# Attention, then a rational feed-forward, on one core: four phases of w made in place, one DMA queue, and a reciprocal by Ln, Exp and a Newton step

## The chip, the core and the metric

One core of one Trainium2 chip runs the whole program. The metric is the device time of one execution in microseconds (us); lower is better. TensorE (PE) multiplies, VectorE (DVE), ScalarE (ACT) and GpSimd (POOL) work on tiles, and SyncE (SP) issues DMA transfers. Each engine takes its instructions in the order in which the program holds them.

## The reference, cut to what matters

Four batches, twelve heads, 448 positions, head size 64; then 1792 tokens through a feed-forward of width 768 to 2048 to 768.

```python
scores = scale * np.matmul(q, k.transpose(0, 1, 3, 2))
scores = np.einsum('bhij,hg->bgij', scores, w_pre)
scores = scores - np.max(scores, axis=-1, keepdims=True)
attn = np.exp(scores)
attn = attn / (np.sum(attn, axis=-1, keepdims=True) + 1e-09)
attn = np.einsum('bhij,hg->bgij', attn, w_post)
x = matmul(attn, v)            # then regrouped to 1792 x 768
h = x @ w_in
P = a[0] + a[1] * h + a[2] * h2 + a[3] * h3
Q = 1.0 + np.abs(b[0]) * np.abs(h) + np.abs(b[1]) * h2
g = P / (Q + 1e-06)
out = g @ w_out
```

## The kernel before, in words

The program has two parts. A small planner (`Plan`, `add`) gets every step with its engine, an estimated duration, what it depends on and a due time `at`; it runs through them once in simulated time, and the order it finds is the order in which each engine gets its instructions. Rings (`Ring`, `R[...]`) stand for buffers that are used again. Nothing of the planner runs on the chip: there, an engine simply waits at its next instruction until what that one needs is there.

**Attention.** There are 16 row tiles, four to a batch. For a tile, `put_qk` multiplies q and k for six pairs of heads (L451), ScalarE or VectorE copies the scores to `st`, and one DMA for each head (`shuffle`, L467, `d<-st`, 210 KB, twelve to a tile) lays them out in `d` so that the heads can be mixed by a matmul. There are two buffers of `d`. `put_pre` mixes the heads (L518, the first matmul that needs the whole shuffled tile), VectorE takes the maxima (L525), ScalarE the exponentials (L534), GpSimd scales the second mixing matrix (L554). `put_post` mixes again (L594), VectorE transposes (L610), `put_av` multiplies by v (L653) and splits the result into a high and a low half, `xs` (L667). At the end of a batch `xs` is stored to a scratch, `x_scr` (L671). The shuffles of a tile run while the tile before is being worked on. Shuffles stand on SyncE's queue; the loads of q (L352), k (L364) and v (L632) of all but the first tiles, and the stores of x, stand on ScalarE's (`bulk(second, ...)`).

**The weights.** w_in and w_out come as one array w of 64-bit floats: 16 rows (f) of 128 x 1536 values. `put_w` makes a quarter of a row (a *piece*, 128 x 384, 64 in all): a load `cr` on SyncE (L380), Abs on ScalarE (L385), a clamp on GpSimd (L390), three integer steps on VectorE (L394, L399, L405), a high half on ScalarE (cast `co`, L235), a low half on GpSimd (L416), and a store to the scratch `w_scr` on SyncE (L419). 36 pieces are due during attention (`W1 = 36`), 28 after it. `put_load_w` loads a whole row of both halves, 1.5 MB, from the scratch (L764); eight rows have room at a time.

**Feed-forward.** 64 units: a unit is one row f of w and one batch b. `put_unit` multiplies x by w_in (18 matmuls, L799, into one of two `ps_s` banks) and later adds g times w_out to six banks (18 matmuls, L873). Between them ScalarE makes four values (L810, L813, L816, L820), VectorE the polynomial P (L823, L826), the denominator (L830), its reciprocal (L833) and the quotient (L836); g is split into a high half (cast, L235 or L237) and a low half (L846). There are two phases of eight rows; within a phase the four batches take turns of eight units. At the end of a turn the six banks are copied to `o` and stored in `o_scr`, or in the second phase added to what was stored (L910) and sent out (L917). x of a batch that is not at hand is loaded again (L780).

What sets the order of the units, of the x tiles held and of the pieces:

```python
    turns = [(0, 3), (0, 0), (0, 1), (0, 2), (1, 2), (1, 1), (1, 0), (1, 3)]
    units = [(c, b, f) for c, b in turns for f in range(CH)]
    held = [0, 1, 2, 3, 3, 2, 4, 5]
    homes = {1: (0, "x"), 2: (1, "xs"), 3: (2, "x"), 4: (0, "x"), 5: (3, "xs")}
```

```python
        if i < W1:
            put_w(f, c, at=T0 + 10.0 + (tau[first[NT - 1]] - T0 - 30.0) * i / W1)
        else:
            put_w(f, c, at=END1 + 26 * UNIT * (i - W1) / (len(pieces) - W1))
```

## Time and profile before

| what | value |
|---|---|
| median of 3 runs | 952.78 us (951.53 to 957.07) |
| profiled execution, its own time | 955.4 us |
| span of the profiled execution | 953.6 us |
| mean granted TensorE clock | 0.958 |
| TensorE matmul, weight load busy | 850.2 us (89%), 649.6 us (68%) |
| VectorE busy | 751.7 us (79%) |
| ScalarE busy | 415.2 us (44%) |
| GpSimd busy | 358.2 us (38%) |
| DMA | 175.32 MB, mean 184 GB/s |

Times are from the start of the span. Busy time is a mean over parts with different limits, so the table alone does not tell what a part waits for. Matmuls are pipelined and their ends modelled; a granted clock of 1.00 is full speed. In rows of waits, what stands behind `<-` is what ended the wait, as inferred from the semaphores; where several things were awaited it is the one that came last.

### The profile page before, as it was taken

What the parts mean: (1) busy time and instruction counts of PE and PEld (TensorE: products, weight loads), DVE (VectorE), ACT (ScalarE), POOL (GpSimd) and SP (SyncE); (2) the same over time, 40 slices, a digit from 0 to 9 for tenths busy, and PEclk for the clock granted to TensorE, in tenths of its full rate; (3) what the DMA queues carried; (4) which work ended last, traced back from release to release, by engine and by line L of the source; (5) the groups of instructions that cost most, each with busy time, mean ns of one, the idle gap of its engine ahead of it and who ended that gap; (6) DMA issues with size and microseconds to landing.
All of it is one profiled execution on the core that took longest, in us unless ns stands there. A gap on an engine that the chain in (4) does not pass through costs nothing.

```text
span 953.6 us, 26592 instructions
## 1 busy us (share of the span) xinstructions
PE 850.2 (89%) x11088; PEld 649.6 (68%) x11088; DVE 751.7 (79%) x1158; ACT 415.2 (44%) x928; POOL 358.2 (38%) x472
## 2 busy tenths in 40 slices
PE   3588889879877998897899899899999999999996
PEld 1245445444535555554689799799999999999995
DVE  4467768768856888686898999999788787887975
ACT  1245544545534656454435645544344233233420
POOL 2255455546435665243525645451111112121110
PEclk9789899999989999899999999999999999999998
DMA  7577768867887677547796536521555230420212
GB/s 239 182 218 217 230 209 282 267 182 237 249 277 225 204 219 248 195 149 276 245 424 240 186 119 232 174 84 39 203 213 190 102 112 20 174 97 1 77 40 77
DMA packets 68119, 175.32 MB, mean 184 GB/s; under 512 B 6336, under 2 KB 47392, under 8 KB 65312
## 3 DMA queue, kind: packets, MB, share of 16 engines
...
q8 instruction: 87, 1.43, 0.6%
...
## 4 chain that ended last, share of the span: by engine, by line
PE 54%; DMA 17%; DVE 16%; issue 6%; POOL 3%; ACT 3%; SPq 1%; POOLq 0%; DVEq 0%; ACTq 0%
PE ps_s L799 17%; PE ps_t L873 11%; DMA d<-st 7%; PE ps_a L873 6%; PE ps_t L518 5%; PE ps_a L594 5%; PE ps_s L451 5%; PE ps_t L653 4%; DVE rc L833 4%; DMA w_scr<-co 3%; DMA kk<-in_k 2%; DVE aa L610 2%; DMA x_scr<-xs 2%; DVE cg L399 2%; POOL cm L390 1%
## 5 line engine op out<-in xcount | busy, mean ns | idle before, releaser
L846 POOL TENSOR_TENSOR g<-rc,g 128x448 fp32r<-128x448 f32 x63 | 76.7, 1218 | 312.6 <-DVE g L237 201.0
L833 DVE RECIPROCAL rc<-sq 128x448 f32<-128x448 f32 x64 | 188.5, 2945 | 1.2
L873 PE MATMUL ps_t<-g,w 128*128 128x448 f32 x768 | 180.2, 366 | 0.1
L518 PE MATMUL ps_t<-d,kpre 64*64 64x448 f32 x720 | 105.6, 605 | 57.8 <-DMA d<-st 24.8
L873 PEld LDWEIGHTS ps_t<-g,w 128*128 128x128 f32 x768 | 144.1, 188 | 12.4 <-POOL g L846 0.5
L594 PEld LDWEIGHTS ps_a<-e,krs 64*32 64x32 f32 x5760 | 81.4, 110 | 89.3 <-issue 39.8
L525 DVE TENSOR_REDUCE nm<-ps_t 128x1 f32<-128x448 f32 x180 | 104.4, 607 | 39.0 <-PE ps_t L518 38.2
L390 POOL TENSOR_SCALAR cm<-cm 128x384 f32<-128x384 f32 x64 | 98.4, 1540 | 78.0 <-ACT cm L385 71.5
L799 PE MATMUL ps_s<-x,w 128*128 128x448 f32 x576 | 123.8, 369 | 3.7 <-DVE m L826 3.7
L799 PE MATMUL ps_s<-xs,w 128*128 128x448 f32 x576 | 122.7, 366 | 3.8 <-DVE m L826 3.5
L534 ACT ACTIVATE e<-ps_t,nm 128x448 f32<-128x448 f32 x180 | 113.0, 636 | 27.8 <-DVE nm L525 19.4
L451 PE MATMUL ps_s<-kk,q 64*64 64x448 f32 x736 | 113.0, 608 | 12.6 <-DMA kk<-in_k 6.7
L610 DVE STREAM_TRANSPOSE aa<-ps_a 128x448 f32<-128x448 f32 (+1 forms) x184 | 106.8, 615 | 19.8 <-PE ps_a L594 19.2
L810 ACT ACTIVATE m<-ps_s,a_sb 128x448 f32<-128x448 f32 x64 | 46.3, 724 | 171.8 <-PE ps_s L799 171.7
L594 PE MATMUL ps_a<-e,krs 64*32 64x112 f32 x5760 | 109.3, 272 | 13.1 <-issue 4.9
L799 PEld LDWEIGHTS ps_s<-x,w 128*128 128x128 f32 x576 | 109.4, 190 | 13.3 <-DVE m L826 4.1
L799 PEld LDWEIGHTS ps_s<-xs,w 128*128 128x128 f32 x576 | 107.7, 188 | 14.2 <-DVE m L826 4.6
L554 POOL TENSOR_SCALAR krs<-kpost,rr 128x64 f32<-128x64 f32 x180 | 89.5, 510 | 68.2 <-DVE rr L545 56.3
L873 PE MATMUL ps_a<-g,w 128*128 128x448 f32 x384 | 97.8, 366 | 0.0
L653 PE MATMUL ps_t<-aa,vv 128*64 128x120 f32 (+1 forms) x1536 | 83.0, 262 | 2.7 <-DVE aa L610 1.6
L416 POOL TENSOR_TENSOR co<-cm,co 128x384 fp32r<-128x384 f32 x64 | 68.3, 1069 | 44.6 <-ACT co L235 44.3
L235 ACT COPY st<-ps_s 120x448 f32<-120x448 f32 (+1 forms) x104 | 52.7, 532 | 73.4 <-PE ps_s L451 60.7
...
## 6 DMA issues: line engine op xcount, KB each, us to landing
...
```

What stands on the lines that cost most here:

```text
L390: nc.gpsimd.tensor_scalar(out=m, in0=m, scalar1=F64_MIN, scalar2=F64_MAX, op0=ALU.max, op1=ALU.min)
L451: nc.tensor.matmul(box["s"][hh][i0:i1, 0:S], lhsT=Q[T][d, pr, i0:i1], rhs=K[b][d, pr, :], start=True, stop=True)
L518: nc.tensor.matmul(box[r if nt == 2 else 0]["t"][64 * c:64 * c + 64, 0:S], lhsT=kpre[p], rhs=Dt[T][p, kb + c if nt == 2 else kb, :], start ...
L525: nc.vector.tensor_reduce(out=nm, in_=box[r]["t"][:, 0:S], axis=AX.X, op=ALU.max, negate=True)
L534: nc.scalar.activation(e, box[r]["t"][:, 0:S], AF.Exp, bias=box[r]["nm"], accum_out=box[0]["sm"][:, r:r + 1])
L554: eng.tensor_scalar_mul(box[r]["kr"], kpost, rr)
L594: nc.tensor.matmul(banks[c]["p"][BT * q_:BT * (q_ + 1), j0:j0 + JT], lhsT=box[r]["kr"][p, m_, :], rhs=box[r]["e"][p, q_ * JT:(q_ + 1) * JT ...
L610: nc.vector.transpose(o, src)
L653: nc.tensor.matmul(t[64 * hf:64 * hf + 64, pr * n:(pr + 1) * n], lhsT=V[b][:, j, g, :], rhs=A[T][:, 3 * (g // G6) + j, 0:n // G5, G5 * (g ...
L799: nc.tensor.matmul(h[:, 0:S], lhsT=W[fi][:, wi, kk * 128:(kk + 1) * 128], rhs=x[:, kk // 3, xj, kk % 3, :], start=(n == 0), stop=(n == 3 * ...
L833: nc.vector.reciprocal(new("rc"), box["vv"])
L873: nc.tensor.matmul(O[key][:, 0:S], lhsT=W[fi][:, wi, DM + m * 128:DM + (m + 1) * 128], rhs=box["g"][:, gi, :], start=(f == 0 and n == 0), ...
```

## The change

Four things are edited.

- **Phases.** The feed-forward has four phases of four rows of w (`PH = 4`); a turn has four units, there are 16 turns, and partial sums go through `o_scr` three times instead of once. x tiles are loaded nine times instead of five.
- **Pieces.** Only the 16 pieces of the first phase are made during attention and go through the scratch. The other 48 are due one to a unit, a phase ahead of use, and are written straight into the buffer of the row (`W[f]`), without store and load.
- **Queue.** All loads of q, k, v and all stores of x go to SyncE's queue, k in six parts instead of three, v in four instead of two, x in twelve to a batch instead of four.
- **Reciprocal.** Ln and Exp(-x) on ScalarE give a first value r, and two VectorE instructions make r * (d * r - 2), the negative of a Newton step; the coefficients a are negated once to make up for the sign. One table load for Ln is placed ahead of the first unit.

```diff
+PH = 4
-    w_scr = [dram.tile([128, 2, WC], F32, name=f"w_scr{f}") for f in range(NF)]
+    w_scr = [dram.tile([128, 2, WC], F32, name=f"w_scr{f}") for f in range(PH)]
...
-    b1_op = add("act", 0.15, lambda: nc.scalar.activation(b1_sb, b_sb[:, 1:2], AF.Abs), [ab_ld], at=40.0)
+    def fit_ab():
+        nc.scalar.activation(b1_sb, b_sb[:, 1:2], AF.Abs)
+        nc.scalar.activation(a_sb, a_sb, AF.Copy, scale=-1.0)
...
-            (nc.scalar if T > 1 else nc.sync).dma_start(out=Q[T], in_=q[T])
+            nc.sync.dma_start(out=Q[T], in_=q[T])
...
-                (nc.scalar if b else nc.sync).dma_start(out=K[b][:, i * n:(i + 1) * n], in_=k[b, :, i * n:(i + 1) * n])
+                nc.sync.dma_start(out=K[b][:, i * n:(i + 1) * n], in_=k[b, :, i * n:(i + 1) * n])
...
         def hi(eng):
-            t = sb["co"].tile([128, 2, CV], F32R, tag="co", name="co")
+            if f < PH:
+                t = sb["co"].tile([128, 2, CV], F32R, tag="co", name="co")
+            else:
+                if c == 0:
+                    W[f] = sb["wr" if f % CH < NR else "wl"].tile([128, 2, WC], F32R, tag="w", name=f"w{f}")
+                t = W[f][:, :, sl]
...
+        if f < PH:
+            home = [R["co"].take()]
+        elif c == 0:
+            home = [op_begin if f % CH < NR else op_rest, w_use[f - CH] if f >= CH else None]
+        else:
+            home = []
...
-                (nc.scalar if b else nc.sync).dma_start(out=V[b][:, 2 * j:2 * j + 2], in_=v[b, :, 2 * j:2 * j + 2])
+                nc.sync.dma_start(out=V[b][:, j], in_=v[b, :, j])
...
-                nc.scalar.dma_start(out=x_scr[b][:, hv, hl], in_=Xs[b][:, hv, hl].bitcast(F32))
+                nc.sync.dma_start(out=x_scr[b][:, hv, hl, p], in_=Xs[b][:, hv, hl, p].bitcast(F32))
...
-        put_k(b, 3, at=tau[first[4 * b - 2]] - 40.0, gap=12.0)
+        put_k(b, 6, at=tau[first[4 * b - 2]] - 40.0, gap=7.0)
...
-    pieces = [(f, c) for f in range(NF) for c in range(NCV)]
-    for i, (f, c) in enumerate(pieces):
-        if i < W1:
-            put_w(f, c, at=T0 + 10.0 + (tau[first[NT - 1]] - T0 - 30.0) * i / W1)
-        else:
-            put_w(f, c, at=END1 + 26 * UNIT * (i - W1) / (len(pieces) - W1))
+    for i in range(PH * NCV):
+        put_w(i // NCV, i % NCV, at=T0 + 10.0 + (tau[first[NT - 1]] - T0 - 40.0) * i / (PH * NCV))
...
+    orders = [(3, 0, 1, 2), (2, 1, 0, 3)]
+    turns = [(c, b) for c in range(NF // PH) for b in orders[c % 2]]
+    units = [(c, b, f) for c, b in turns for f in range(PH)]
+    held = [0, 1, 2, 3, 3, 2, 4, 5, 5, 4, 6, 7, 7, 6, 8, 9]
...
         def cubic():
+            if u == 0:
+                nc.scalar.preload_act_table_set("natural_log_exp_and_others")
...
-        def rec():
-            nc.vector.reciprocal(new("rc"), box["vv"])
+        def log():
+            nc.scalar.activation(box["ua"], box["vv"], AF.Ln)
+
+        def seed():
+            nc.scalar.activation(new("rc"), box["ua"], AF.Exp, scale=-1.0)
+
+        def step1():
+            nc.vector.tensor_mul(box["vv"], box["vv"], box["rc"])
+
+        def step2():
+            nc.vector.scalar_tensor_tensor(
+                out=box["rc"], in0=box["vv"], scalar=-2.0, in1=box["rc"], op0=ALU.add, op1=ALU.mult)
...
+    for u in range(len(units)):
+        i = u + PH * NCV
+        if i < NF * NCV:
+            put_w(i // NCV, i % NCV, at=END1 + UNIT * u + 2.0, since=END1 + UNIT * u - 6.0)
```

Some lines of the changed kernel are called by their number below: L852 is `step1`, L855 `step2`, L846 and L849 are Ln and Exp there, L936 the addition of partial sums.

Where the instructions move is shown at two places. The first is SyncE's queue in the middle of the attention part, in the kernel before (`d<-st` is a shuffle, `cr` a load and `w_scr` a store of a piece; L467, L380, L419):

```order
L467 DMA d<-st 10x12x448 x6
L380 DMA cr<-in_w 128x768
L467 DMA d<-st 10x12x448 x3
L419 DMA w_scr_121<-co 256x1x384
L467 DMA d<-st 10x12x448
L380 DMA cr<-in_w 128x768 x2
L419 DMA w_scr_121<-co 256x1x384
```

And in the changed kernel (`vv`, `kk` and `q` are parts of v, k and q; L489 is the shuffle there):

```order
L654 DMA vv<-in_v 128x768
L387 DMA cr<-in_w 128x768
L489 DMA d<-st 10x12x448 x4
L369 DMA kk<-in_k 128x448
L431 DMA w_scr_117<-co 256x1x384
L489 DMA d<-st 10x12x448 x2
L357 DMA q<-in_q 128x768
L489 DMA d<-st 10x12x448 x2
L369 DMA kk<-in_k 128x448
L431 DMA w_scr_117<-co 256x1x384
```

Between the shuffles there now stand parts of q, k and v, and fewer pieces. Before, those loads stood in ScalarE's order, between its own work, here also from the middle of the attention part:

```order
L632 DMA vv<-in_v 128x1536
L385 ACTIVATE cm<-cr 128x384
L534 ACTIVATE e,sm<-ps_t,nm 128x448 x2
L352 DMA q<-in_q 128x768
L235 CAST co<-cm 128x384
```

In the changed kernel ScalarE's order holds no load of q, k or v and no store of x.

The second place is VectorE's order in the feed-forward, with pieces among the units. Before, in the first phase:

```order
L833 RECIPROCAL rc<-sq 128x448
L394 TENSOR_SCALAR cm<-cm 128x384
L836 SCALAR_TENSOR_TENSOR rc<-m,a_sb,rc 128x448
L399 SCALAR_TENSOR_TENSOR cg<-cr,cm 128x384
L823 TENSOR_TENSOR m<-m,ps_s 128x448
L405 SCALAR_TENSOR_TENSOR cm<-cr,cg 128x384
```

In the changed kernel, in the second phase:

```order
L406 SCALAR_TENSOR_TENSOR cg<-cr,cm 128x384
L412 SCALAR_TENSOR_TENSOR cm<-cr,cg 128x384
L852 TENSOR_TENSOR sq<-sq,rc 128x448
L401 TENSOR_SCALAR cm<-cm 128x384
L855 SCALAR_TENSOR_TENSOR rc<-sq,rc 128x448
L406 SCALAR_TENSOR_TENSOR cg<-cr,cm 128x384
L859 SCALAR_TENSOR_TENSOR rc<-m,a_sb,rc 128x448
L412 SCALAR_TENSOR_TENSOR cm<-cr,cg 128x384
```

The reciprocal is gone, two instructions stand ahead of the quotient (L859) that both need `rc` of ScalarE, and steps of pieces stand between them.

## Rows read from the trace of the kernel before

**Rows 1.** Busy time by stretch: each engine (instructions), TensorE clock, DMA share, GB/s

```profile
core 0: us, PE busy (x) PEld busy (x) DVE busy (x) ACT busy (x) POOL busy (x), PEclk, DMA share, GB/s
30.00:466.00 436.00, 368.92 (x8728) 213.44 (x8721) 323.01 (x690) 218.23 (x578) 217.30 (x357) 0.93 0.71 224
390.00:420.00 30.00, 29.73 (x780) 18.05 (x776) 24.70 (x54) 17.22 (x47) 12.38 (x28) 1.00 0.50 154
466.00:602.00 136.00, 131.44 (x634) 119.98 (x635) 127.91 (x147) 69.83 (x129) 65.67 (x50) 0.99 0.68 251
602.00:946.00 344.00, 340.22 (x1672) 313.22 (x1670) 288.25 (x307) 123.62 (x216) 69.73 (x58) 1.00 0.29 104
```

**Rows 2.** Groups of TensorE, 30 to 466 us: busy, mean ns | idle before, releasers

```profile
L518 PE MATMUL ps_t<-d,kpre 64*64 64x448 f32 x719 | 105.6, 605 | 46.4 <-DMA d<-st 13.5 <-issue 12.3 <-DMA cr<-in_w 11.1
```

**Rows 3.** Time line of TensorE, 170 to 205 us: start, length, [idle before <-releaser]

```profile
170.87 2.38 PE L518 MATMUL ps_t<-d,kpre 64*64 64x448 f32 x8 [5.09 <-DMA w_scr<-co]
...
175.36 0.98 PE L518 MATMUL ps_t<-d,kpre 64*64 64x448 f32 x8
...
204.52 0.88 PE L518 MATMUL ps_t<-d,kpre 64*64 64x448 f32 x2 [4.09 <-issue]
```

**Rows 4.** Waits of SyncE's queue, 20 to 466 us: total us, times, longest

```profile
SPq L380 <- DVE cm L405: 25.1, 6, 14.2
SPq L467 <- DMA kk<-in_k: 24.1, 6, 6.8
SPq L467 <- DMA vv<-in_v: 21.7, 5, 7.4
...
SPq L467 <- DMA x_scr<-xs: 14.9, 4, 7.3
SPq L467 <- DMA q<-in_q: 13.9, 3, 5.7
```

**Rows 5.** Chain that ended last, 154 to 171 us: start, length, what

```profile
154.27 6.41 DMA kk<-in_k
...
160.75 5.28 DMA d<-st
...
166.53 4.31 DMA w_scr<-co
```

**Rows 6.** Groups, ScalarE's first step of a piece, 30 to 466 us

```profile
L385 ACT ACTIVATE cm<-cr 128x384 f32<-128x384 f32 x43 | 23.9, 558 | 70.8 <-DMA cr<-in_w 58.2 <-POOL co L416 12.5
```

**Rows 7.** Groups of VectorE, 470 to 602 us

```profile
L833 DVE RECIPROCAL rc<-sq 128x448 f32<-128x448 f32 x18 | 53.0, 2944 | 0.4
L830 DVE TENSOR_TENSOR sq<-sq,ua 128x448 f32<-128x448 f32 x18 | 13.7, 760 | 0.1
L399 DVE SCALAR_TENSOR_TENSOR cg<-cr,cm 128x384 int32<-128x384 int32 x16 | 12.9, 806 | 0.3
L826 DVE SCALAR_TENSOR_TENSOR m<-m,a_sb,ps_s 128x448 f32<-128x448 f32 x18 | 12.1, 672 | 0.0
L836 DVE SCALAR_TENSOR_TENSOR rc<-m,a_sb,rc 128x448 f32<-128x448 f32 x17 | 11.4, 672 | 0.1
L823 DVE TENSOR_TENSOR m<-m,ps_s 128x448 f32<-128x448 f32 x18 | 10.8, 601 | 5.1 <-ACT ua L816 5.1
L405 DVE SCALAR_TENSOR_TENSOR cm<-cr,cg 128x384 int32<-128x384 int32 x16 | 10.4, 653 | 0.1
L394 DVE TENSOR_SCALAR cm<-cm 128x384 int32<-128x384 int32 x16 | 9.4, 589 | 1.9 <-POOL cm L390 1.9
```

**Rows 8.** Line L830, 470 to 602 us: shortest/median/longest ns

```profile
L830 DVE TENSOR_TENSOR sq<-sq,ua x18: 609/622/1187, 472.8 to 599.9; 128x448 f32<-128x448 f32 x18
```

**Rows 9.** Groups of VectorE, whole span: additions to o, casts of g

```profile
L237 DVE CAST g<-rc 128x448 fp32r<-128x448 f32 x36 | 14.1, 393 | 3.2
L910 DVE TENSOR_TENSOR o<-ps_t,o 128x448 f32<-128x448 f32 x16 | 9.9, 621 | 2.8 <-PE ps_t L873 2.6
```

**Rows 10.** Groups of ScalarE, whole span: attention's Exp, the unit's Identity

```profile
L534 ACT ACTIVATE e<-ps_t,nm 128x448 f32<-128x448 f32 x180 | 113.0, 636 | 27.8 <-DVE nm L525 19.4 <-DVE rr L545 8.0
L820 ACT ACTIVATE sq<-sq,c_sb,b_sb 128x448 f32<-128x448 f32 x64 | 49.2, 768 | 0.0
```

More of the change, by code (lines that the diff above doesn't have):

```diff
@@ L351, in load @@
             Q[T] = sb["q"].tile([128, H // 2, TQ], F32, tag="q", name="q")
-            (nc.scalar if T > 1 else nc.sync).dma_start(out=Q[T], in_=q[T])
-        q_ld[T] = bulk(T > 1, 0.63, load, [R["q"].take()], at=at, nbytes=128 * H // 2 * TQ * 4)
+            nc.sync.dma_start(out=Q[T], in_=q[T])
+        q_ld[T] = bulk(0.63, load, [R["q"].take()], at=at, nbytes=128 * H // 2 * TQ * 4)
     def put_k(b, parts, at, gap=0.8):
@@ L368, in put_k, with put_w @@
         for i in range(parts):
-            k_ld[b].append(bulk(b > 0, 0.5, load(i), [free] + k_ld[b][:1], at=at + gap * i, nbytes=128 * n * S * 4, since=at + gap * i - 4.0))
+            k_ld[b].append(bulk(0.45, load(i), [free] + k_ld[b][:1], at=at + gap * i, nbytes=128 * n * S * 4, since=at + gap * i - 4.0))
     w_done = {f: [] for f in range(NF)}
-    def put_w(f, c, at):
+    w_ld, w_use = {f: [] for f in range(NF)}, {f: [] for f in range(NF)}
+    W = {}
+    def put_w(f, c, at, since=0.0):
         sl = slice(c * CV, (c + 1) * CV)
@@ L419, in store @@
             nc.sync.dma_start(out=w_scr[f][:, :, sl], in_=box["o"].bitcast(F32))
[L421 removed]
+        ld = add("sp", 0.45, load, [R["cr"].take()], at=at - 5.0, extra=dma(128 * CV * 8), since=max(since, at - 14.0))
         o1 = add("act", act(CV), mag, [ld, R["cm"].take()], at=at)
[L423 removed]
+        o2 = add("pool", 1.54, clamp, [o1], at=at)
         o3 = add("dve", dve(CV, True), shift, [o2], at=at)
[L425 to L426 removed]
+        o4 = add("dve", 0.59, top, [o3, R["cg"].take()], at=at)
+        o5 = add("dve", 0.57, tail, [o4], at=at)
         R["cg"].uses[-1].append(o5)
         R["cr"].uses[-1].append(o5)
[L429 removed]
+        if f < PH:
[4 more added lines that the diff above has]
+            home = []
+        o6 = add(copies(CV, on=ON["w_hi"]), 0, hi, [o5] + [x for x in home if x], at=at, after=w_ld[f][:1] if f >= PH else ())
         o7 = add(subs(CV, on=ON["w_lo"]), 0, lo, [o6], at=at)
         R["cm"].uses[-1].append(o7)
[L432 to L434 removed]
+        if f < PH:
+            o8 = add("sp", 0.57, store, [o7], at=at, extra=dma(128 * CV * 8), late=2.0)
+            R["co"].uses[-1].append(o8)
+            w_done[f].append(o8)
+        else:
+            w_ld[f].append(o6)
+            w_ld[f].append(o7)
     qk_op, shuf, evac = {}, {}, {}
@@ L636, in put_v @@
         v_ld[b] = []
-        for j in range(NJ // 2):
-            v_ld[b].append(bulk(b > 0, 0.63, load(j), [free] + v_ld[b][:1], at=at + 10.0 * j, nbytes=2 * 128 * H * D * 4, since=at + 10.0 * j))
+        for j in range(NJ):
+            v_ld[b].append(bulk(0.63, load(j), [free] + v_ld[b][:1], at=at + 8.0 * j, nbytes=128 * H * D * 4, since=at + 8.0 * j))
     Xs = {}
@@ L689, in put_av @@
         if T % 4 == 3:
-            for i in range(2):
-                o = bulk(True, 0.6, store(i), x_done[b, hv], at=at + 5.0 + 5.0 * (2 * i + hv),
-                         nbytes=128 * 3 * S * 4, late=1.0, since=at + 4.0 + 5.0 * (2 * i + hv))
+            for i in range(6):
+                o = bulk(0.45, store(i // 3, i % 3), x_done[b, hv], at=at + 5.0 + 1.6 * (2 * i + hv),
+                         nbytes=128 * S * 4, late=2.0, since=at + 4.0 + 1.6 * (2 * i + hv))
                 x_st.setdefault(b, []).append(o)
@@ L748, in mixed_attention_then_rational_ffn @@
     op_rest = add("sp", 0.0, rest, [left_ops, op_begin], at=-100.0)
-    turns = [(0, 3), (0, 0), (0, 1), (0, 2), (1, 2), (1, 1), (1, 0), (1, 3)]
-    units = [(c, b, f) for c, b in turns for f in range(CH)]
-    held = [0, 1, 2, 3, 3, 2, 4, 5]
-    homes = {1: (0, "x"), 2: (1, "xs"), 3: (2, "x"), 4: (0, "x"), 5: (3, "xs")}
-    W, X, O = {}, {}, {}
-    w_ld, x_ld, m2_op, o_ev = {}, {}, {}, {}
-    w_use = {f: [] for f in range(NF)}
+    orders = [(3, 0, 1, 2), (2, 1, 0, 3)]
+    turns = [(c, b) for c in range(NF // PH) for b in orders[c % 2]]
+    units = [(c, b, f) for c, b in turns for f in range(PH)]
+    held = [0, 1, 2, 3, 3, 2, 4, 5, 5, 4, 6, 7, 7, 6, 8, 9]
+    homes = {n: (turns[held.index(n)][1], "xs" if n in (2, 5, 6, 9) else "x") for n in range(1, 10)}
+    X, O = {}, {}
+    x_ld, m2_op, o_ev = {}, {}, {}
     x_use = {0: R["xs"].uses[B - 1]}
@@ L888, in put_unit @@
         w_use[fi].append(prev)
-        if f == CH - 1:
+        if f == PH - 1:
             for m0 in range(0, KD, 2):
@@ L933, in put_unit @@
                     R["xo"].uses[-1].append(s_)
-                    if not c:
-                        o_st.setdefault(b, []).append(s_)
+                    o_st.setdefault((c, b), []).append(s_)
     for f in range(NR):
         put_load_w(f, at=END1 - 30)
-    for f in range(NR, CH):
+    for f in range(NR, PH):
         put_load_w(f, at=END1 - 10 + f)
-    for n, turn in ((1, 0), (2, 1), (3, 2), (4, 5), (5, 6)):
-        put_load_x(n, at=END1 + UNIT * CH * turn + 1)
-    for u, (c, b, f) in enumerate(units):
-        if u // CH == NF // CH * B // 2:
-            put_load_w(CH + f, at=END1 + UNIT * (u - CH + 2))
+    for n in homes:
+        put_load_x(n, at=END1 + UNIT * PH * (held.index(n) - 1) + 1)
+    for u in range(len(units)):
+        i = u + PH * NCV
+        if i < NF * NCV:
+            put_w(i // NCV, i % NCV, at=END1 + UNIT * u + 2.0, since=END1 + UNIT * u - 6.0)
         put_unit(u)
```

43 lines of the change are left out of this document (16 added, 27 removed).

## The prediction, made before the changed kernel was run

> **What bounds the kernel now.** First the split into stages [rows 1]: busy time of each engine, then the granted TensorE clock, DMA share and rate. The attention part ends near 466 us, the feed-forward part near 946 us, and 8 us of last adds and stores follow.
>
> In the feed-forward part TensorE is the bound. From 602 to 946 us it is busy 340.2 of 344 us, with 1672 matmul records, 0.2035 us each; a unit has 36, so 7.33 us, and 64 units need 469 us of the 480 that lie between 466 and 946. So some 11 us of waiting are there to be had and no more. From 466 to 602 us VectorE is nearly full beside it, 127.9 of 136 us (94%): what it gains or loses there matters.
>
> In the attention part nothing is full. From 30 to 466 us TensorE is busy 368.9 of 436 us, idle 67, and its mean granted clock is 0.93. In a window in the same part with a DMA share of 0.50 instead of 0.71 it is busy 29.7 of 30 us at clock 1.00. Where it idles is shown by the groups of instructions [rows 2]: 46.4 of the 67 us stand ahead of L518, the first matmul on a tile of shuffled scores, put down to the shuffle `d<-st` itself or to a transfer near it. The time line [rows 3] shows what one such wait is: once a tile, three to five us, and the next eight matmuls take 2.38 us instead of 0.98, since the clock has dropped. That second price is in the mean clock: 0.07 of 436 us is 30 us.
>
> Why the shuffle is late is read from SyncE's queue [rows 4]. Shuffles wait there for transfers that ScalarE issued: 24.1 us behind k, 21.7 behind v, 14.9 behind x stores, 13.9 behind q, 74.6 us in all; loads of w pieces hold the queue another 25.1 us until VectorE gives a buffer back. The chain [rows 5] has one case in full: a load of k from 154.27 to 160.7, at whose end a shuffle is issued, then the store of a w piece, and the matmul at 170.87. By 466 us, 43 of the 64 pieces have passed through ScalarE, which sat idle 58.2 us for their loads [rows 6]; it also makes exponentials and evacuates scores.
>
> **The change: attention.** (a) Pieces. 16 belong to the first phase, and in the new order a few more stand ahead of the feed-forward: about 19 instead of 43, 24 fewer. Each has a load and a store of 0.39 MB (128 rows of 384 x 8 bytes): 19 MB less, of 224 GB/s over 436 us or 98 MB [rows 1]. (b) Queue. 45 loads and stores go from ScalarE to SyncE, in smaller parts: 101 in all there (16 q, 21 k, 16 v, 48 x). SyncE issues more, but has no long transfer of another queue to wait for; a shuffle now stands behind at most some parts of 0.2 to 0.4 MB. At the 251 GB/s of the busiest stretch [rows 1] that is 0.8 to 1.6 us each, against 6.4 us for the k load of [rows 5]. What is queued behind a wait for x (x stores wait for VectorE's subtraction) is again a shuffle, and TensorE waits for that.
>
> What is gained is bounded below by nothing (the same megabytes of q, k, v and x still pass the same engines in front of shuffles) and above by all that stands before L518 with all of the clock, 46 + 30 = 77 us. I take two thirds of the idle time, 31 us, since the waits behind ScalarE's transfers are three quarters of those 99.7 us and the fewer pieces take most of the rest, and half of the clock, 15 us: **-46 us**. The remaining 21 us of idle time (67 less 46) I leave.
>
> **The change: feed-forward.** VectorE's durations where pieces run beside units [rows 7]: a unit was 0.601 + 0.672 + 0.760 + 2.944 + 0.672 = 5.65 us. The reciprocal goes; a product (L852) and a scalar-tensor-tensor (L855) come. Neither is in the trace. The product is like L830, 0.760 on average, 0.609 at least and 1.187 at most [rows 8]; the other is like L836, 0.672. A unit is then 4.14 us, 1.51 less. A piece costs 0.589 + 0.806 + 0.653 = 2.05 us.
>
> From the second phase each turn of four units adds six results of 0.621 us [rows 9]; there are 12 such turns, and there were four. The new order has 34 casts (0.393 us) and 18 subtractions (taken as 0.62) of g on VectorE for 64 units. So the 32 units of the second and third phase, with a piece each: 32 x 6.19 = 198, 48 adds 30, 17 casts 7, nine subtractions 6, in sum 240 us, against 32 x 7.33 = 235 for TensorE. VectorE becomes the bound there. At a busy share of 0.97 (between the 0.94 of [rows 1] and full) it takes 247 us, 13 more than TensorE alone. The first 16 units: 99 for units and pieces, 15 for copies and g, 114 us, 117 at that share, equal to TensorE's 117: nothing. The last 16 have no pieces: 86 of 117, nothing.
>
> Ln and Exp are new on ScalarE. They are bounded by L534 (0.636, an Exp) and L820 (0.768, from SBUF) [rows 10]; 0.64 each is 1.3 us a unit. ScalarE was busy 69.8 of 136 us with 17.6 units (634 records / 36) [rows 1], 4.0 us a unit; 5.3 of 7.33 remains hidden, also at 0.768. GpSimd, 65.7 of 136 us, gets about one piece a unit as before and fewer subtractions: hidden. The chain through a unit gives up 2.94 us and gets 0.64 + 0.64 + 0.76 + 0.67 = 2.71 with two more hand-overs: no change. Transfers: nine x loads of 2.75 MB and 72 of o at 0.46 MB, in 480 us, with the pieces' loads some 85 MB or 177 GB/s, below the 251 that the first 136 us bear; hidden behind matmuls, and if an x load came late, a turn waits for what is missing of its 11 us. For the beginning, with a table load for Ln, I allow 4 us.
>
> So feed-forward 469 + 13 + 4 = 486 against 480: **+6 us**. Bounds: 469, if VectorE never holds TensorE (-11), and 533 (the second rival).
>
> **Sum.** -46 + 6 = -40. The profiled execution had 955.4 us with a span of 953.6; it lies 2.6 us above the median of the runs, 952.78. 955.4 - 40 = 915.4, or 912.8 on the median: I say **915 us**.
>
> **The rules weighed.** SyncE's waits [rows 4] say that transfers of another queue hold the shuffles. The Trainium skill (DMA: Bandwidth & Descriptors, "Issuing engines are not separate DMA queues") says that transfers issued from several engines run on the same 16 DMA engines and interleave, so that several issuers save only issue time. By that rule moving them gains no transfer time and only the fewer pieces count, the first rival below; the rows bear the rule out for the rate, but they show waits in the queue, which the rule does not speak of.
>
> L830, with two operands in SBUF, is 0.609 at least and 1.187 at most. The Trainium skill (SBUF — State Buffer, "Who interferes with whom") says that a VectorE instruction with two SBUF inputs contends with a GpSimd instruction that reads SBUF. By it both new instructions are exposed, as the reciprocal was not, which is the second rival; L830's spread agrees, but L836, also with two SBUF inputs, stays at a mean of 0.672, the same as L826 with a PSUM operand.
>
> **Rivals.** 1. *The shuffles stay late* (0.15): q, k, v and x stand in one line with them, and 74.6 us of waiting turn into as much queueing. Of the idle time before L518 only the 11.1 us under w loads go, with a like share of the clock (7 us): -18 + 6, **943 us**, up to 953 if the longer line costs 10. For it: the bytes are the same. Against: the window of [rows 1] in which neither pieces nor bulk loads were dense ran at 99%.
>
> 2. *VectorE holds TensorE* (0.13), slower. If both new instructions take 1.187, a unit has 5.08 us instead of 4.14; the middle 32 units need 270 / 0.97 = 278 us, 44 over TensorE, the first 16 another 16 over. Feed-forward 469 + 60 + 4 = 533, +53: 955 - 46 + 53 = **962 us**. It decides once the two cost about 2.2 us together instead of 1.43, or a wait for Ln and Exp in VectorE's order costs the same 0.8 us a unit. For it: 240 of 235 us without any wait. Against: at 94% full it held TensorE back by 4.6 of 136 us only.
>
> 3. *The attention part runs free* (0.17): at the pace of the light window, 780 records in 30 us, its 8728 take 336 us instead of 436. All of that would need a share of 0.50, which the 79 MB that are left (224 GB/s over 436 us, less 19 MB) in 336 us do not give: 235 GB/s, above the 224 of now; three quarters of it, -73 + 6, is **888 us**.
>
> 4. *Nothing moves* (0.05): gain and loss cancel, 948 to 958.
>
> **How the numbers follow.** My forecast has 0.50, its own range 895 to 937 (attention -25 to -60, feed-forward 0 to +15). Range **880 to 953**: it takes in the third rival and most of the first, and leaves out the second. A measurement of this kernel can tell some 0.5% from no change, 948 to 958. Faster by more: 0.50 + 0.17 + two thirds of the first rival = 0.77; within: 0.09; slower: 0.14, the second rival and a remainder.
>
> **What would show it.** Right: before L518 15 us of idle time or less; a clock over 0.95 and an attention end near 420 us; no SyncE wait behind k, v, q of over 3 us; in the second and third phase VectorE over 95% busy and TensorE a few per cent idle; L852 near 0.76. Wrong: an attention end past 450, TensorE idle over 30 us in the middle phases, or ScalarE in idle waits for w loads there.

## The result, and the profile after

The changed kernel takes **914.18 us** (median of 4 runs, 907.13 to 915.77) where the kernel before took 952.15 us (950.01 to 957.07) on the same chip: a ratio of 0.958, interval 0.952 to 0.964. The profiled execution had 915.77 us, its span 913.9 us, the mean granted TensorE clock was 0.970. The prediction was 915 us. Here and below, a ratio leaves out executions that took over 1.5% longer than the shortest of the same kernel, and a median takes them all.

Busy time by stretch of the changed kernel, which answers to [rows 1] (attention, feed-forward, and of the latter first the second and third phase, then the first and the last; columns as there):

```profile
core 0: us, PE busy (x) PEld busy (x) DVE busy (x) ACT busy (x) POOL busy (x), PEclk, DMA share, GB/s
30.00:426.00 396.00, 353.83 (x8710) 211.38 (x8708) 290.54 (x622) 191.61 (x519) 144.57 (x305) 0.95 0.65 203
426.00:906.00 480.00, 472.35 (x2316) 433.40 (x2311) 396.27 (x659) 282.57 (x520) 188.31 (x140) 1.00 0.50 171
543.00:778.00 235.00, 230.26 (x1122) 211.22 (x1121) 210.88 (x352) 141.54 (x263) 106.09 (x78) 0.99 0.53 181
426.00:543.00 117.00, 114.09 (x566) 103.96 (x562) 101.03 (x167) 82.51 (x155) 59.13 (x44) 1.00 0.53 184
778.00:906.00 128.00, 128.00 (x632) 118.22 (x630) 84.37 (x143) 58.52 (x103) 23.10 (x18) 1.00 0.41 140
```

Attention ends 40 us earlier, at 426 instead of 466 us; the feed-forward part takes the 480 us that it took. In attention TensorE is idle 42.2 us (396 - 353.8) instead of 67.1, 24.9 less, and the same matmuls keep it busy 15.1 us less (353.8, was 368.9), at a clock of 0.95 instead of 0.93: together the 40 us.

TensorE's groups in attention show which idle time went and which came. The kernel before, 30 to 466 us (its other rows; L518 is in [rows 2]), then the changed one, 30 to 426 us, where L473 is the q k product, L540 the first mixing matmul and L616 the second (the product with v has 2.7 us of idle time before and 2.2 after):

```profile
L594 PE MATMUL ps_a<-e,krs 64*32 64x112 f32 x5760 | 109.3, 272 | 13.1 <-issue 4.9 <-DVE rr L545 4.5 <-DVE aa L610 2.9
L451 PE MATMUL ps_s<-kk,q 64*64 64x448 f32 x712 | 108.3, 605 | 4.9 <-ACT st L235 3.2 <-DVE st L237 1.7
```

```profile
L616 PE MATMUL ps_a<-e,krs 64*32 64x112 f32 x5760 | 106.3, 269 | 11.0 <-issue 6.9 <-DVE aa L632 2.7 <-POOL krs L576 0.6
L473 PE MATMUL ps_s<-kk,q 64*64 64x448 f32 x708 | 100.4, 577 | 21.3 <-ACT st L236 18.6 <-DVE st L238 1.5 <-issue 1.2
L540 PE MATMUL ps_t<-d,kpre 64*64 64x448 f32 x712 | 95.3, 568 | 7.7 <-DMA d<-st 3.8 <-issue 1.4 <-DVE xs L689 0.8
```

Ahead of the shuffled tile 46.4 us have become 7.7. But ahead of the q k product 4.9 have become 21.3: TensorE now waits for ScalarE to clear the banks of scores. The shuffles are on time. SyncE no longer stands behind another queue's transfers; the experiments below show what that alone is worth, and what the fewer pieces are worth. Its waits, 20 to 426 us (columns as in [rows 4]), hold no row for k, v, q or x:

```profile
SPq L489 <- ACT st L236: 68.6, 32, 7.7
SPq L489 <- ACT e L556: 65.2, 46, 7.6
SPq L387 <- DVE cm L412: 21.4, 2, 13.0
```

These are the longest. SyncE waits mostly for ScalarE, by the profile for its copies of scores (`st`) and its exponentials (`e`).

Why ScalarE is late is in its waits (20 to 426 us) and its time line. L392 is its first step on a piece of w, L236 its copies and casts:

```profile
ACT xs L236 <- PE ps_t L675: 63.6, 24, 7.9
ACT cm L392 <- DMA cr<-in_w: 44.2, 15, 5.8
ACT e L556 <- DVE nm L547: 38.9, 33, 6.9
```

```profile
266.63 0.55 ACT L392 ACTIVATE cm<-cr 128x384 f32<-128x384 f32 x1 [5.77 <-DMA cr<-in_w]
267.08 0.44 ACT L236 CAST xs<-ps_t 128x360 fp32r<-128x360 f32 x1
267.42 0.54 ACT L236 COPY st<-ps_s 120x448 f32<-120x448 f32 x1
```

At 260.9 us ScalarE comes to L392 and stands 5.77 us until the load of the piece has landed. The copy of scores that frees TensorE's bank is two places behind it. TensorE's time line at the same place:

```profile
263.49 0.93 PE L540 MATMUL ps_t<-d,kpre 64*64 64x448 f32 x8
268.01 2.43 PE L473 MATMUL ps_s<-kk,q 64*64 64x448 f32 x8 [3.59 <-ACT st L236]
270.37 1.46 PE L616 MATMUL ps_a<-e,krs 64*32 64x112 f32 x64
271.76 2.75 PE L675 MATMUL ps_t<-aa,vv 128*64 128x120 f32 x48
274.44 0.98 PE L540 MATMUL ps_t<-d,kpre 64*64 64x448 f32 x8
```

It waits 3.59 us, and the next eight matmuls take 2.43 us instead of the 0.98 that eight take at 274.44. Fifteen such waits of ScalarE are 44.2 us (before, [rows 6] had 58.2 us of idle time at 43 pieces).

In the second and third phase (543 to 778 us) VectorE is 90% busy, TensorE 98%. VectorE's largest groups there, and a stretch of its time line (start, length); they answer to [rows 7, 8, 9]:

```profile
L859 DVE SCALAR_TENSOR_TENSOR rc<-m,a_sb,rc 128x448 f32<-128x448 f32 x31 | 25.4, 819 | 0.4
L855 DVE SCALAR_TENSOR_TENSOR rc<-sq,rc 128x448 f32<-128x448 f32 x31 | 23.6, 760 | 0.8
L406 DVE SCALAR_TENSOR_TENSOR cg<-cr,cm 128x384 int32<-128x384 int32 x30 | 21.1, 704 | 0.5
L852 DVE TENSOR_TENSOR sq<-sq,rc 128x448 f32<-128x448 f32 x31 | 21.0, 676 | 9.2 <-ACT rc L849 9.1
...
L869 DVE TENSOR_TENSOR g<-rc,g 128x448 fp32r<-128x448 f32 x15 | 11.5, 765 | 0.4 <-ACT g L236 0.2
```

```profile
603.03 0.62 DVE L855 SCALAR_TENSOR_TENSOR rc<-sq,rc 128x448 f32<-128x448 f32 x1
603.57 0.68 DVE L839 SCALAR_TENSOR_TENSOR m<-m,a_sb,ps_s 128x448 f32<-128x448 f32 x1
604.16 0.93 DVE L859 SCALAR_TENSOR_TENSOR rc<-m,a_sb,rc 128x448 f32<-128x448 f32 x1
605.01 0.61 DVE L843 TENSOR_TENSOR sq<-sq,ua 128x448 f32<-128x448 f32 x1
```

Each of these instructions begins before the one ahead of it has ended: L839 at 603.57, when L855 runs to 603.65; L859 at 604.16, when L839 runs to 604.25. So the sum of the fifteen groups of this stretch, 231 us, is more than the 210.9 us for which the engine was busy.

### The profile page after: what moved, and what is told of

It is laid out like the page before. It is cut to its first block, busy times and chain, and to the rows that moved or that the text cites. A ratio compares the mean times of both kernels' runs of the same rounds, so it can differ in the third digit from the quotient of the medians.

```text
span 913.9 us, 26984 instructions
## 1 busy us (share of the span) xinstructions
PE 837.3 (92%) x11088; PEld 648.1 (71%) x11088; DVE 699.1 (76%) x1297; ACT 479.0 (52%) x1048; POOL 339.9 (37%) x455
## 3 DMA queue, kind: packets, MB, share of 16 engines
q8 instruction: 87, 1.43, 0.6%
## 4 chain that ended last, share of the span: by engine, by line
PE 54%; DVE 22%; DMA 8%; issue 7%; ACT 4%; POOL 3%; SPq 2%; DVEq 0%; ACTq 0%; POOLq 0%
PE ps_s L810 13%; PE ps_t L899 10%; PE ps_a L616 7%; PE ps_s L473 7%; PE ps_t L675 7%; PE ps_t L540 6%; PE ps_a L899 5%; DMA d<-st 4%; DVE aa L632 2%; DVE cg L406 2%; DVE rc L859 2%; DVE sq L843 2%; DVE cm L412 2%; DVE rc L855 2%; DVE m L836 2%
## 5 line engine op out<-in xcount | busy, mean ns | idle before, releaser
L899 PE MATMUL ps_t<-g,w 128*128 128x448 f32 x768 | 176.4, 366 | 0.0
L616 PEld LDWEIGHTS ps_a<-e,krs 64*32 64x32 f32 x5760 | 79.8, 108 | 83.5 <-issue 35.6
L397 POOL TENSOR_SCALAR cm<-cm 128x384 f32<-128x384 f32 x64 | 102.7, 1608 | 93.3 <-ACT cm L392 88.8
L473 PE MATMUL ps_s<-kk,q 64*64 64x448 f32 x736 | 105.8, 583 | 29.7 <-ACT st L236 20.2
L810 PE MATMUL ps_s<-xs,w 128*128 128x448 f32 x576 | 124.0, 370 | 5.5 <-DVE m L839 5.5
L869 POOL TENSOR_TENSOR g<-rc,g 128x448 fp32r<-128x448 f32 x46 | 59.9, 1302 | 178.9 <-DVE g L238 103.6
L810 PE MATMUL ps_s<-x,w 128*128 128x448 f32 x576 | 122.6, 366 | 2.1 <-DVE m L839 2.1
L810 PEld LDWEIGHTS ps_s<-xs,w 128*128 128x128 f32 x576 | 109.0, 190 | 16.1 <-DVE m L839 7.0
L810 PEld LDWEIGHTS ps_s<-x,w 128*128 128x128 f32 x576 | 108.0, 188 | 11.9 <-DVE m L839 2.9
L616 PE MATMUL ps_a<-e,krs 64*32 64x112 f32 x5760 | 106.3, 269 | 11.0 <-issue 6.9
L540 PE MATMUL ps_t<-d,kpre 64*64 64x448 f32 x720 | 97.0, 572 | 16.9 <-DMA d<-st 13.0
L576 POOL TENSOR_SCALAR krs<-kpost,rr 128x64 f32<-128x64 f32 x180 | 83.0, 476 | 61.4 <-DVE rr L567 48.7
L675 PE MATMUL ps_t<-aa,vv 128*64 128x120 f32 (+1 forms) x1536 | 86.5, 269 | 2.2 <-issue 1.4
L428 POOL TENSOR_TENSOR w<-cm,w 128x384 fp32r<-128x384 f32 x48 | 53.9, 1126 | 89.6 <-ACT w L236 89.5
L473 PEld LDWEIGHTS ps_s<-kk,q 64*64 64x64 f32 x736 | 31.4, 139 | 77.1 <-ACT st L236 34.1
L675 PEld LDWEIGHTS ps_t<-aa,vv 128*64 128x64 f32 x1536 | 79.2, 140 | 8.6 <-issue 7.3
L236 ACT COPY st<-ps_s 120x448 f32<-120x448 f32 (+1 forms) x98 | 49.8, 532 | 55.5 <-PE ps_s L473 32.1
```

The costliest lines, as they stand in the source:

```text
L397: nc.gpsimd.tensor_scalar(out=m, in0=m, scalar1=F64_MIN, scalar2=F64_MAX, op0=ALU.max, op1=ALU.min)
L473: nc.tensor.matmul(box["s"][hh][i0:i1, 0:S], lhsT=Q[T][d, pr, i0:i1], rhs=K[b][d, pr, :], start=True, stop=True)
L540: nc.tensor.matmul(box[r if nt == 2 else 0]["t"][64 * c:64 * c + 64, 0:S], lhsT=kpre[p], rhs=Dt[T][p, kb + c if nt == 2 else kb, :], start ...
L576: eng.tensor_scalar_mul(box[r]["kr"], kpost, rr)
L616: nc.tensor.matmul(banks[c]["p"][BT * q_:BT * (q_ + 1), j0:j0 + JT], lhsT=box[r]["kr"][p, m_, :], rhs=box[r]["e"][p, q_ * JT:(q_ + 1) * JT ...
L675: nc.tensor.matmul(t[64 * hf:64 * hf + 64, pr * n:(pr + 1) * n], lhsT=V[b][:, j, g, :], rhs=A[T][:, 3 * (g // G6) + j, 0:n // G5, G5 * (g ...
```

## The experiments

Ratios are to the kernel before, run beside it on the same chip (medians of 955.7 to 957.7 us). "Attention end" is the start of the first feed-forward matmul in the profiled execution: 465.9 us before, 426.4 after. Where the idle time of TensorE is counted from 32 us on, it is to leave out the wait for the very first shuffled tile, which ends between 26 and 30 us and is no part of the rows of before and after either. A profile is one execution, and the attention end varies from one to the next: it is 424.5 us when the changed kernel is run again (*c0*), and 419.75 in *e3*, which changes attention by no more than one small step of ScalarE.

**What the queue is worth, what the rest.** *e1_queue_back* is the changed kernel with q, k, v and x on ScalarE's queue, in the parts of before:

```diff
-        return add("sp", dur, fn, deps, at=at, extra=dma(nbytes), **more)
+        return add("act" if second else "sp", dur, fn, deps, at=at, ...
...
-                nc.sync.dma_start(out=K[b][:, i * n:(i + 1) * n], in_=k[b, :, i * n:(i + 1) * n])
+                (nc.scalar if b else nc.sync).dma_start(out=K[b][:, i * n:(i + 1) * n], ...
```

> The changed kernel, but q, k, v and x go through ScalarE's queue in the parts of before. Theory (most of the gain is that shuffles no longer wait behind transfers of another queue): attention ends some 25 us later, near 450 us, SyncE waits behind k, v, q and x again for 50 to 75 us, idle time of TensorE before the first mixing matmul back to 30 us or more, in all 935 to 942 us. Rival (the fewer pieces alone did it): attention ends by 430 us, 912 to 920 us. The feed-forward stays at 480 us by both.

931.1 us, ratio 0.9735 (0.968 to 0.979), attention end 440.2, 10 us earlier than expected. SyncE's waits behind the other queue are back, 45.2 us in these rows:

```profile
SPq L489 <- DMA x_scr<-xs: 13.7, 5, 5.0
SPq L489 <- DMA vv<-in_v: 12.5, 4, 4.9
SPq L489 <- DMA q<-in_q: 10.8, 5, 4.4
SPq L489 <- DMA kk<-in_k: 8.2, 2, 5.8
```

and with them 26.1 us ahead of the shuffled tile (from 32 us on):

```profile
L540 PE MATMUL ps_t<-d,kpre 64*64 64x448 f32 x712 | 98.0, 584 | 26.1 <-DMA d<-st 14.2 <-ACT e L556 7.5 <-DMA x_scr<-xs 3.6
```

The queue matters; the rest of the change alone is worth 2.7%, a little more than the theory said. The feed-forward part takes 480 us here too, so that all of it is attention, where the rest of the change means fewer pieces (18 through ScalarE, 43 before).

*e4_queue_alone* is the reverse: the kernel before with only the queue and the part sizes of the change (the edit of e1 the other way round).

> The kernel before, with nothing but the queue and the parts changed. Theory: attention ends some 25 us earlier, near 440 us, 925 to 932 us; SyncE has no wait behind k, v, q or x of over 3 us. Rival (the fewer pieces alone did it, or queueing takes the place of the waits): attention end unchanged, 948 to 956 us.

Its four times scatter from 918.02 to 938.33 us, too far for a ratio. *e10_queue_alone_again*, the same kernel, measured it a second time:

> The kernel before with one thing of the change alone: all transfers on SyncE's queue, in the changed kernel's parts. A second, longer measurement of the run e4_queue_alone, whose times lay from 918.02 to 938.33 us. Theory: the queue alone is worth the 18 us by which TensorE's last attention matmul came earlier there (465.9 to 447.6 us): ratio near 0.98, time near 935 us, first feed-forward matmul near 447 us. Rival: the 918 us of the one short time is the kernel's own, the queue is nearly all of the change's gain and the pieces in place add little: ratio below 0.97.

930.8 us, ratio 0.9713 (0.966 to 0.977); attention end 447.6 in its profile, which is of its longest execution (933.92 us), and as the theory has it. The ratio lies between the two: 2.9% instead of 2, and not nearly all of the gain. So either half alone gives under 3%, and both together 4 to 5%. The profile of e10, from 32 us on:

```profile
L518 PE MATMUL ps_t<-d,kpre 64*64 64x448 f32 x712 | 98.3, 577 | 27.3 <-DMA d<-st 8.3 <-ACT e L534 5.0 <-DMA w_scr<-co 4.6
```

Here the shuffles' waits behind k, v, q and x are gone (2.4 us in all, was 74.6), and 27.3 us stay, with the 43 pieces of before still going through; in e1 there are fewer pieces, the waits are back, and 26.1 stay. So of the 46.4 us the queue alone takes 19.1, the rest alone 20.3, and both together take 38.7: the halves add up. The same holds for the attention end, which comes 18.3 us earlier with the queue, 25.7 with the rest and 39.5 with both. At which group the idle time stands is less certain than its sum: e4, the same kernel as e10, has 36.6 us ahead of the shuffled tile and 8.3 ahead of the q k product, e10 27.3 and 17.2, and both have 54 us of idle time in all. Whether a piece delays TensorE by its transfers in SyncE's queue or by its steps on ScalarE and VectorE, no run separates.

*e2_pieces36* leaves the changed kernel as it is, but sends 36 pieces through the scratch in attention and makes 28 in place:

```diff
+NS = 9
...
-        if f < PH:
+        if f < NS:
...
-    for i in range(PH * NCV):
+    for i in range(NS * NCV):
```

> The changed kernel, but nine rows of w (36 pieces) are made during attention and go through the scratch, 28 in place. Theory: the pieces are the smaller part of the gain, attention ends 12 to 18 us later, in all 926 to 932 us; the feed-forward, with 20 pieces fewer, gains at most 5 us. Rival 1 (pieces do it all): attention ends near 460 us, 945 us or more. Rival 2 (queue does it all): 910 to 916 us.

921.0 us, ratio 0.9605 (0.956 to 0.966). Attention end 436.9, 10.5 us later than in the changed kernel (12 to 18 were expected); what follows takes 483.4 us instead of 487.5. Twenty pieces cost about half a microsecond each in attention, and give a fifth of a microsecond each back.

*e6_coarse_parts* keeps all transfers on SyncE, but in the larger parts of before:

```diff
-            for i in range(6):
+            for i in range(2):
...
-        put_k(b, 6, at=tau[first[4 * b - 2]] - 40.0, gap=7.0)
+        put_k(b, 3, at=tau[first[4 * b - 2]] - 40.0, gap=12.0)
```

> The changed kernel, all on SyncE's queue, but in the parts of before: k in three, v in two, x in four. Theory (what counts is that nothing is waited for across queues; a part of 0.8 MB instead of 0.4 delays a shuffle by a microsecond or two): 0 to 6 us longer. Rival (the small parts are what makes one queue bearable): 12 us or more longer, with idle time before the first mixing matmul over 25 us.

918.5 us, ratio 0.9565 (0.951 to 0.962), beside 0.9519 (0.948 to 0.956) of *c0_changed_again*, the changed kernel run beside it:

> The changed kernel itself, as the measure for the two runs beside it: ratio to the kernel before 0.955 to 0.963 by every theory.

c0 had 911.8 us and repeats the reading of above (attention end 424.5, 22.4 us ahead of L473, 6.9 ahead of L540). The size of the parts is worth about 0.5%, and as the intervals overlap not even that is sure; in e1 and e10, where the parts change with the queue, most of the effect is the queue's.

**What the reciprocal is worth.** *e3_reciprocal_back* puts VectorE's reciprocal in the place of Ln, Exp and the two steps:

```diff
-            nc.scalar.activation(box["ua"], box["vv"], AF.Ln)
...
-            nc.scalar.activation(new("rc"), box["ua"], AF.Exp, scale=-1.0)
...
+            nc.vector.reciprocal(new("rc"), box["vv"])
```

> The changed kernel, but with VectorE's reciprocal instead of Ln, Exp and the Newton step. Theory (VectorE has no room for it beside a piece a unit): a unit takes VectorE 5.65 + 2.05 + 0.93 us in the middle phases, 282 us and 0.97 busy against 235 for TensorE, and 138 against 117 in the first phase; feed-forward 60 to 75 us longer, 970 to 990 us. Rival (TensorE stays the bound, as it was with pieces and reciprocal in the first 136 us of before): 912 to 925 us.

927.1 us, ratio 0.9706 (0.965 to 0.976); from the attention end (419.75) to the end of the span it takes 502.1 us, against 487.5 in the changed kernel, 14.7 more. A miss: 60 to 75 were expected, and the time is 2 us above what the rival allowed. Its stretch from 420 to 908 us:

```profile
420.00:908.00 488.00, 472.51 (x2277) 426.21 (x2277) 469.98 (x546) 230.31 (x423) 199.71 (x152) 1.00 0.49 167
```

VectorE is 96% busy over the whole part, TensorE 97%. The expectation summed mean durations, which here too are more than the engine's busy time, and left out that the planner, with VectorE's steps dearer, gives casts and subtractions of g to ScalarE and GpSimd.

**The new wait.** ScalarE comes to L392 before the piece has landed. *e5_early_loads* makes the load due earlier:

```diff
-        ld = add("sp", 0.45, load, [R["cr"].take()], at=at - 5.0, ...
+        ld = add("sp", 0.45, load, [R["cr"].take()], at=at - (20.0 if f < PH else 5.0), ...
```

> The changed kernel, but the pieces of the attention part are due for loading 20 us ahead of their first step instead of 5. Theory (what is left in attention is ScalarE standing before a piece whose load is not there, with the score copies that TensorE needs behind it, two of the three longest stalls): ScalarE's 44 us of waits for these loads fall under 15, TensorE's 19 us before the score matmuls under 11, attention ends 7 to 12 us earlier, 1% off the time. Rival (another wait ends at the same moment, or the loads now stand in front of shuffles): within 0.5% of the changed kernel.

911.95 us, ratio 0.9531 (0.949 to 0.957), no different from c0. ScalarE's wait for `cr` is still 47.0 us: the planner brought the first step forward together with the load, so the distance between the two stayed (from the issue of a load to the step 6.4 us at the median of 17 pieces, 6.0 in the changed kernel). The edit did not do what it was meant to. In its profile (of its longest execution, 918.97 us, from 32 us on) idle time has moved all the same:

```profile
L473 PE MATMUL ps_s<-kk,q 64*64 64x448 f32 x712 | 103.5, 583 | 9.2 <-ACT st L236 7.4 <-DVE st L238 1.8
L540 PE MATMUL ps_t<-d,kpre 64*64 64x448 f32 x712 | 96.8, 574 | 14.0 <-DMA w_scr<-co 5.5 <-DVE xs L689 5.4 <-DMA d<-st 1.3
```

Ahead of the q k product 21.3 us are 9.2, though ScalarE waits for its pieces as long as before, and ahead of the shuffled tile 7.7 are 14.0. It fits that less of ScalarE's wait reaches TensorE where shuffles come later.

*e7_late_first_step* tells the planner instead that the step may start 10 us after its load at the earliest:

```diff
-        o1 = add("act", act(CV), mag, [ld, R["cm"].take()], at=at)
+        o1 = add("act", act(CV), mag, [ld, R["cm"].take()], at=at, late=10.0 if f < PH else 0.0)
```

> The changed kernel, but ScalarE's first step on a piece of the attention part stands 10 us of planned time behind the landing of its load; the run with early loads had only moved load and step forward together, by priority, with the same 5 to 7 us between them. Theory (ScalarE standing before unlanded pieces holds up the score copies behind it): ScalarE's waits for these loads fall from 44 to 51 us to under 12, TensorE's 19 to 21 us before the score matmuls to under 11, attention ends 7 to 12 us earlier, ratio to the changed kernel 0.987 to 0.993. Rival (another wait ends at the same moment): the ScalarE waits fall, the time stays within 0.5% of the changed kernel.

**905.63 us** (903.66 to 908.83), ratio 0.9474 (0.945 to 0.950), attention end 418.4. From load to step there are now 13.8 us at the median, ScalarE's waits for `cr` are down to one, and TensorE's groups from 30 to 418 us are:

```profile
ACT cm L392 <- DMA cr<-in_w: 4.5, 1, 4.5
```

```profile
L616 PE MATMUL ps_a<-e,krs 64*32 64x112 f32 x5760 | 105.8, 268 | 15.1 <-issue 10.3 <-DVE aa L632 3.0 <-POOL sm L563 0.9
L540 PE MATMUL ps_t<-d,kpre 64*64 64x448 f32 x712 | 98.0, 584 | 13.6 <-DMA d<-st 9.5 <-DMA kk<-in_k 1.3 <-issue 1.2
L473 PE MATMUL ps_s<-kk,q 64*64 64x448 f32 x704 | 97.4, 574 | 3.6 <-DVE st L238 1.9 <-ACT st L236 1.7
```

The 21.3 us ahead of the q k product are 3.6, and about 10 of those 17.7 us come back ahead of L540 and L616; some 8 us are kept against the first profile of the changed kernel, 6 against c0. This is the fastest version of the study, about 0.5% below the changed kernel (c0), less than expected, and as the two intervals overlap the gain in time is not sure. What is sure is that the wait ahead of L473 goes with ScalarE's.

*e8_late_and_x_early* adds closer spacing of the x stores (0.9 us instead of 1.6):

```diff
-                o = bulk(0.45, store(i // 3, i % 3), x_done[b, hv], at=at + 5.0 + 1.6 * (2 * i + hv),
+                o = bulk(0.45, store(i // 3, i % 3), x_done[b, hv], at=at + 4.0 + 0.9 * (2 * i + hv),
```

> As the run beside it, and the twelve stores of a batch's x follow each other in 0.9 us of planned time instead of 1.6. Theory (a cast of the next batch waits once or twice for these stores, 6 to 8 us each time): 3 to 6 us less than the run beside it. Rival (denser stores stand in front of shuffles): equal or longer.

907.97 us, ratio 0.9506 (0.948 to 0.953): equal or longer, as the rival has it.

*e9_before_late* gives the kernel before the same cure (`late=6.0`):

```diff
-        o1 = add("act", act(CV), mag, [ld, R["cm"].take()], at=at)
+        o1 = add("act", act(CV), mag, [ld, R["cm"].take()], at=at, late=6.0 if at < END1 else 0.0)
```

> The kernel before, but ScalarE's first step on a piece of the attention part stands 6 us of planned time behind the landing of its load. Theory (in the kernel before TensorE waits for shuffles held behind other transfers, and ScalarE's 58 us of waits for pieces are hidden behind that): within 1% of the kernel before. Rival (those 58 us were themselves the loss, and fewer pieces help since there are fewer such waits): 930 to 942 us.

976.72 us, ratio 1.0229 (1.020 to 1.026): about 2% slower, which neither theory nor rival had. ScalarE's waits for `cr` are nearly gone here too (2.0 us), but attention ends at 488.1, and TensorE's idle time before the shuffled tile (32 to 488 us) has grown from 46.4 to 63.7 us:

```profile
L518 PE MATMUL ps_t<-d,kpre 64*64 64x448 f32 x712 | 101.4, 607 | 63.7 <-DMA cr<-in_w 29.1 <-DMA d<-st 15.8 <-issue 10.9
```

One such wait, on the time lines of SyncE's queue and of TensorE:

```profile
153.74 2.22 SPq L467 DMA_DIRECT2D d<-st  x2
165.68 0.34 SPq L380 DMA_DIRECT2D cr<-in_w  x1
```

```profile
SPq L380 <- DMA x_scr<-xs: 9.7, 1, 9.7
```

```profile
167.72 1.08 PE L594 MATMUL ps_a<-e,krs 64*32 64x112 f32 x64
179.49 1.77 PE L518 MATMUL ps_t<-d,kpre 64*64 64x448 f32 x8 [10.69 <-DMA cr<-in_w]
```

SyncE issues nothing from 156 to 165.7 us: for 9.7 us (its waits from 140 to 182 us, the second fence) it stands at the load of a piece until an x store of ScalarE's queue is done. The shuffles come behind that, and TensorE waits 10.69 us. *e11_queue_and_late* asks whether it is the queue that spoils the cure: the same edit on e10's kernel.

> The kernel of e10_queue_alone_again with ScalarE's first step on a piece of w planned 6 us later after its load in attention, the same edit that made the kernel before 2.3% slower (e9_before_late). Theory: there the gain was eaten by SyncE, which stood behind transfers of ScalarE's queue; with those waits gone the edit gains here as it did in the changed kernel (-6 us in attention): 0.5 to 1% below e10_queue_alone_again, ScalarE's waits for piece loads from about 33 us to under 10. Rival: the edit suits only pieces that are made in place, and with all 64 pieces through scratch it costs time whatever the queue: 1 to 2.5% above e10_queue_alone_again.

928.66 us, ratio 0.973 (0.968 to 0.978), against 0.9713 (0.966 to 0.977) of e10: neither gain nor loss, between the two expectations. The loss needs ScalarE's queue, so much is shown; whether there is a gain of e7's size, 0.5%, can't be told, as each ratio is known to about 0.5%. ScalarE's own waits at L385 fell to 5.8 us there (28.7 in e10), and 25.0 us stayed ahead of the shuffled tile (27.3 in e10). Attention ended at 436.2 us, 11 us before e10's, but this profile is of the shortest execution (922.07 us) and that one of the longest. Why the edit reorders the kernel before so that it loses 22 us in attention, beyond this one place, is open.

## Why the prediction was right

**The bound of attention.** Right. Idle time was forecast to fall by 31 us and the time that a low clock costs by 15. Measured: 24.9 us of idle time, and 15.1 us less busy time for the same matmuls. The clock came out at 0.95, just the mark that it was to pass, and attention ended at 426 us, for "near 420". That the sum came out within 1 us of 915 is luck: attention gave 39.5 us where 46 were forecast, the feed-forward part cost nothing where it was to cost 6, and the two errors cancel. The direction, and that nearly all of the gain is in attention, are not luck.

**Where the idle time goes.** Ahead of the shuffled tile it is 7.7 us, under the 15 that would show it right; the forecast of two thirds was too low there, it is five sixths. What the prediction didn't see is the wait that came in its place, +16.4 us ahead of L473, behind ScalarE at its pieces: 38.7 us less, 16.4 more and 2.6 less elsewhere make the 24.9. [Rows 6] had shown 58.2 us of that wait before; the prediction used them only as a sign of late transfers, and left the 21 us of other idle time as they were. The one case that it followed in full, the matmul at 170.87 us of [rows 3] and [rows 5], shows ScalarE at a piece too:

```profile
169.68 0.51 ACT L235 CAST co<-cm 128x384 fp32r<-128x384 f32 x1 [6.15 <-DMA w_scr<-co]
170.10 0.63 ACT L534 ACTIVATE e<-ps_t,nm 128x448 f32<-128x448 f32 x1
170.87 0.28 PEld L518 LDWEIGHTS ps_t<-d,kpre 64*64 64x64 f32 x2 [5.33 <-ACT e L534]
```

ScalarE stood 6.15 us at the cast of a piece, and the exponential behind it ended at 170.73 us. The chain of [rows 5] ends with the store of a piece instead, landed at 170.84; no matmul reads that store, and the weight load ahead of the matmul is put down to the exponential. The two ended 0.1 us apart, so that the case does not show a late shuffle alone. With the shuffles late, ScalarE's wait ran beside TensorE's; with them on time it is what TensorE waits for. e7 shows this: take ScalarE's wait away and the 21.3 us fall to 3.6.

**The reason given for the queue.** "Three quarters of 99.7 us" was put down to ScalarE's transfers, as if waits of SyncE turned into TensorE's one for one. e10 takes away nearly all of the 74.6 us, and 19.1 us of the 46.4 go (9.8 in e4); e1 has the fewer pieces without it, and 20.3 go. So the queue gives half at most of the 38.7 us, not three quarters, and the fewer pieces at least as much. The sum was near because the change does both, not because of that share.

**The first rival**, that shuffles stay late in one line, is refuted by the 7.7 us. Its rule was from the Trainium skill (DMA: Bandwidth & Descriptors, "Issuing engines are not separate DMA queues"): several issuers save issue time only. For the rate the runs agree: e10, with the megabytes of before in one queue, has 235 GB/s in attention, and the kernel before 224. The time is another matter: the queue alone is worth 2.9% (e10), and what went with it are the 74.6 us for which the shuffles stood, by the profile, behind transfers of another engine. Of such waits the rule does not speak, and the measurement decides. Why SyncE must wait for a transfer that a shuffle doesn't read, no run shows.

**Feed-forward.** Forecast +6, measured 0 (480 us). The step that failed is the term of +13 us for VectorE in the second and third phase, by which VectorE becomes the bound at a busy share of 0.97. It was busy 210.9 of 235 us, 90% and not "over 95%". The sum of durations was nearly right, 240 us for 32 units; by the same way of summing the trace has 231 for about 31 (1122 records, 36 to a unit). What was wrong is to take that sum for busy time: successive instructions overlap, 20 of 231 us or 9%, and a sum of means counts that twice. [Rows 7] could have told it: its eight groups add up to 133.7 us in a window of 132 us. Within the sum, L852 and L855 together were right (1.44 for 1.43 us), L859 took 0.819 instead of 0.672, and L401, L406 and L412, a piece, 1.78 instead of 2.05. TensorE waits for VectorE (L810 for m) for 4.7 us in the two phases and 7.7 in the whole part, which is all of its idle time there; before, it was idle 8.3 us of the 480 ([rows 1]). So the 13 us for VectorE and the 4 for the beginning became less than 8, as much as there had been. Ln and Exp cost 0.58 us each on ScalarE; VectorE waits 9.1 us for them in the two phases, and none of TensorE's idle time is put down to them. One sign named for being wrong is there, if small: ScalarE waits 6.9 us for loads of w in the middle phases.

**The second rival** (VectorE holds TensorE) needed 2.2 us for L852 and L855 together; they took 1.44 in the middle phases. The spread that it feared is there in single instructions. All 64 of L852:

```profile
L852 DVE TENSOR_TENSOR sq<-sq,rc x64: 608/624/1446, 437.1 to 897.3; 128x448 f32<-128x448 f32 x64
```

With a median of 624 ns the long ones are few. e3 shows how near the bound is: with the reciprocal back VectorE is 96% full and the part 14.7 us longer.

**The third rival** (attention runs free) did not come: 42 us of idle time stayed, and the rate was 203 GB/s. e7's end at 418 is as far as these edits got.
